# Reordering the operand sums and halves of a seven-product matmul layer, moving some to GpSimd, and loading its first output weights later

## The chip, the cores and the metric

The kernel runs on one core of a Trainium2 chip. The core has a matrix engine (TensorE, PE in the profile, with its weight loads as PEld), three engines for elementwise work (VectorE or DVE, ScalarE or ACT, GpSimd or POOL), and SyncE (SP), whose queue issues the DMAs here. Each engine runs its own instructions in program order and waits on semaphores for the others. The metric is the time of one execution in microseconds (us), the median of several.

## The reference

Three stages follow one another: decayed linear attention, then two feed-forward layers over all 3072 tokens. Everything is float32.

```python
def _attn_ref(q, k, v):                    # 4 x 8 heads x 768 x 64
    for t in range(S):
        state = gamma * state + k[:, :, t] (x) v[:, :, t]
        y[:, :, t] = scale * q[:, :, t] @ state

def _moe_ref(x, w_in, w_out):              # 512 -> 2048 -> 512
    h = x @ w_in
    return (h * np.cos(h)) @ w_out

def _moe2_ref(x, w_gate, w_val, w_out):    # 512 -> 1536 -> 512
    g = x @ w_gate
    silu = g * (1.0 / (1.0 + np.exp(-g)))
    return (silu * (x @ w_val)) @ w_out
```

## The kernel before

Attention and the first feed-forward layer are interleaved and take the first 615 us; the change does not touch them. The tokens are cut into six blocks of 512. Float32 matmuls are done in three passes: each operand is split into a rounded high half (written by ScalarE) and the low half that is left (written by VectorE as a subtraction), and high x high, low x high and high x low are added up in PSUM.

The second layer, from line 680 on, works on pairs of token blocks, three pairs in all, and uses a scheme of seven products in place of eight for a product of 2x2 blocks. The operands of the seven products P1 to P7 are the blocks B11, B21 and B22 themselves and four combinations T1 to T4. The combinations are made in place, one from the other, by subtractions (`g_sum`, line 718): T1 replaces B11's place (slot 0), T2 replaces T1's, T3 goes to slot 1, T4 to slot 2 and needs T2. So the sums have an order, and a place may only be overwritten once its earlier content was split. `g_split` writes the high halves on ScalarE (line 725) and the low halves on VectorE (line 727); with the default `qs` both do it for two chunks, so one call is two instructions on each engine.

The work of a pair runs over 12 *halves* t (36 over all pairs). A half is seven input products of six matmuls each, in the order P1, P2, P4 of the half before, P5, P6, P3, P7 (line 680, `product`). Its results are read out of PSUM: P1 and P5 are copied by ScalarE (857, 874), P6 too (884), and VectorE adds P2, P3 and P7 to these copies (862, 888, 899). Line 899 reads the bank X after P7. P4 of the same half, which runs as the third product of the next half, adds to that bank and so has to wait for line 899. Then ScalarE's sigmoid and VectorE's multiplication (700, 701, 703) form the gated activation in a `raw` tile.

Four halves make a *group* (nine groups, numbered c = 0 to 8, three to a pair; `last` is 8). While the input products of group c run, the output products of group c - 1 (`out_event`, line 766, 14 of six matmuls each, two for each of seven operands) are put between them: `queue` hands one out after P4, P6 and P3, and after P7 in the second and fourth half. Their results are added up by ScalarE or VectorE (775, 777). After the last half the output products of group 8 follow one another without input products between them: the *tail*.

What the change moves is the hand-written placing of `g_sum` and `g_split` in this interleaving: `at(t, name)` is called after the product `name` of half t, h is the half's number in its group, and g = c - 1 is the group whose operands are being made. `one` and `two` name the first and the second of a group's two chunks. Operand work of the token side (`x_sum`, `x_hi`, `x_lo`, lines 631 to 641) is placed by `x_plan`, and falls mainly around the start of each pair, groups 3 and 6.

The weights of the input products come half by half by DMA (`fetch_half`, line 658) in two parts of 1024 and 768 KB: part 0 may be loaded early, part 1 waits for P4 of the half two before. The weights of the output products come in pieces of 512 KB (`fetch_wo`, line 669) into three buffers. All DMAs are issued by SP in program order; the order of these calls in the loop is the order of its queue. The last output products of the first layer, two units, run between the products of the first half (`outs`).

Of the kernel before, what the change touches and what calls it, by code (L numbers as in the profile page):

```python
# [16 lines left out]
ALU = mybir.AluOpType  # L17
# [20 lines left out]
GQ = 2  # L38
# [54 lines left out]
def fused(ctx: ExitStack, tc: tile.TileContext, qkv, w1, w2, consts, out):  # L93
    nc = tc.nc
# [555 lines left out]
    def fetch_half(t, part):  # L650
        if t < len(halves):
            p, q, half = halves[t]
            if part:
                place = Place(w2pool[0], f"b{t % 2}")
                wh[t, part] = place, place.tile([P, 3, 2, 256], "wh")
            else:
                wh[t, part] = want([P, 4, 2, 256], "wh")
            nc.sync.dma_start(out=wh[t, part][1].bitcast(F32), in_=w2d[3 * q + half][part])
# [5 lines left out]
    def fetch_wo():  # L664
        g, n = divmod(next_wo[0], len(ORDER))
        if g < len(groups2):
            next_wo[0] += 1
            wo[g, n] = gpool.tile([P, GQ, 2, 256], F32R, tag="g", name="wo")
            nc.sync.dma_start(
                out=wo[g, n].bitcast(F32).rearrange("p q a c -> p q (a c)"),  # L670
                in_=wod[groups2[g][1]][ORDER.index(order_of(g)[n])],
            )
# [38 lines left out]
    def raw_of(g, qi, slot):  # L711
        p, r = groups2[g]
        return raw[p, GQ * r + qi][1].bitcast(F32)[:, slot]

    def g_sum(g, name, qs=range(GQ)):
        dst, x, y = {"T1": (0, 1, 0), "T2": (0, 3, 0), "T3": (1, 3, 1), "T4": (2, 2, 0)}[name]
        for i in qs:
            nc.vector.tensor_tensor(out=raw_of(g, i, dst), in0=raw_of(g, i, x), in1=raw_of(g, i, y), op=ALU.subtract)  # L718

    def g_split(g, name, qs=range(GQ)):  # L720
        if (g, name) not in opnd:
            opnd[g, name] = want([P, GQ, 2, T], "go")
        t, slot = opnd[g, name][1], SLOT[name]
        for i in qs:
            nc.scalar.activation(out=t[:, i, 0], in_=raw_of(g, i, slot), func=AF.Copy)  # L725
        for i in qs:
            nc.vector.tensor_tensor(  # L727
                out=t[:, i, 1], in0=raw_of(g, i, slot), in1=t[:, i, 0].bitcast(F32), op=ALU.subtract
            )
        if name == "T4":  # L730
            p, r = groups2[g]
            for i in qs:
                raw[p, GQ * r + i][0].give()
# [53 lines left out]
    def second_layer():  # L787
        def flush(n=0):
            for f in later[:len(later) - n]:
                f()  # L790
            del later[:len(later) - n]

        def last_of(t, name):
            p, q, half = halves[t]
            if (q, half) == (M2 // 2 - 1, 1):
                xo[p, PIECES[name][2]][0].give()

        def p4(t):
            x = pst.pop(("X", t))
            n = len(later)  # L800
            product(t, "P4", x, False)
            last_of(t, "P4")
            take_c(t, 1, 0, x)
            flush(len(later) - n)

        queue = []
        both, one, two = range(GQ), range(1), range(1, GQ)
        last = len(groups2) - 1

        def at(t, name):  # L810
            c, h = divmod(t, 2 * GQ)
            g = c - 1
            if name == "P4" and h == 0 and g >= 0:
                queue.extend((g, k) for k in range(14))
                g_split(g, "B21")
            if g >= 0:
                for step, *args in {
                    (0, "P3"): [(g_sum, g, "T1"), (g_split, g, "T1")],
                    (1, "P6"): [(g_sum, g, "T2"), (g_split, g, "T2")],
                    (2, "P2"): [(g_split, g, "B22")],  # L820
                    (2, "P7"): [(g_sum, g, "T3"), (g_split, g, "T3")],
                    (3, "P6"): [(g_sum, g, "T4"), (g_split, g, "T4")],
                }.get((h, name), []):
                    step(*args)
            if c < last:
                if (h, name) == (3, "P7"):
                    g_split(c, "B11")
            else:
                for step, *args in {
                    (2, "P7"): [(g_split, c, "B11", one), (g_sum, c, "T1", one)],  # L830
                    (3, "P2"): [(g_split, c, "T1", one)],
                    (3, "P4"): [(g_split, c, "B21", one), (g_sum, c, "T2", one)],
                    (3, "P5"): [(g_split, c, "T2", one), (g_sum, c, "T3", one)],
                    (3, "P6"): [(g_split, c, "B22", one), (g_sum, c, "T4", one)],
                    (3, "P3"): [(g_split, c, "B11", two), (g_split, c, "T3", one)],
                    (3, "P7"): [(g_sum, c, "T1", two), (g_split, c, "T1", two), (g_split, c, "T4", one)],
                }.get((h, name), []):
                    step(*args)
            if queue and name in ("P4", "P6", "P3") + (("P7",) if h % 2 else ()):
                out_event(*queue.pop(0))  # L840

        for t, (p, q, half) in enumerate(halves):
            x_steps = x_plan.get(t, [])

            def prepare(n):
                for _ in range(n):
                    for step, *args in x_steps.pop(0) if x_steps else []:
                        step(*args)

            def event(name, ps, start):  # L850
                product(t, name, ps, start)
                last_of(t, name)

            X = pst["X", t] = ps_h.tile([P, T], F32, tag="h", name="X")
            event("P1", X, True)
            p1 = tile_t("p1")
            nc.scalar.activation(out=p1, in_=X, func=AF.Copy)
            flush()
            prepare(1)
            Y = ps_a.tile([P, T], F32, tag="a", name="Y")  # L860
            event("P2", Y, True)
            nc.vector.tensor_tensor(out=p1, in0=Y, in1=p1, op=ALU.add)
            take_c(t, 0, 0, p1)
            fetch_half(t + 1, 0)
            prepare(1)
            at(t, "P2")
            if t:
                p4(t - 1)
            fetch_half(t + 1, 1)
            at(t, "P4")  # L870
            Z = ps_a.tile([P, T], F32, tag="a", name="Z")
            event("P5", Z, True)
            p5 = tile_t("p5")
            nc.scalar.activation(out=p5, in_=Z, func=AF.Copy)
            flush()
            prepare(1)
            if outs:
                outs.pop(0)()
            prepare(1)
            at(t, "P5")  # L880
            event("P6", X, False)
            wh[t, 0][0].give()
            u2 = tile_t("u2")
            nc.scalar.activation(out=u2, in_=X, func=AF.Copy)
            prepare(1)
            at(t, "P6")
            event("P3", Z, False)
            nc.vector.tensor_tensor(out=u2, in0=Z, in1=u2, op=ALU.add)
            take_c(t, 0, 1, u2)
            prepare(1)  # L890
            if outs:
                outs.pop(0)()
                for _ in range(3):
                    fetch_wo()
            flush()
            prepare(1)
            at(t, "P3")
            event("P7", X, False)
            nc.vector.tensor_tensor(out=p5, in0=X, in1=p5, op=ALU.add)  # L899
            take_c(t, 1, 1, p5)  # L900
            while x_steps:
                prepare(1)
            at(t, "P7")
        p4(len(halves) - 1)
        flush()
        assert not queue
        for k in range(14):
            out_event(last, k)
            for step, *args in {
                0: [(g_split, last, "B21", two)],  # L910
                1: [(g_sum, last, "T2", two), (g_split, last, "T2", two)],
                3: [(g_sum, last, "T3", two), (g_split, last, "B22", two)],
                5: [(g_split, last, "T3", two), (g_sum, last, "T4", two)],
                7: [(g_split, last, "T4", two)],
            }.get(k, []):
                step(*args)

# [7 lines left out]
    o2, o3, two = (ps_o, "o2"), (ps_o, "o3"), [(ps_a, "a")] * 2  # L925
# [11 lines left out]
    for i in range(CPB):  # L937
        attn_at[21 + 2 * i], attn_at[22 + 2 * i] = scores_of(8 + i), [(attn_both, 8 + i)]
        for j in range(3, NB):
            n, c = 2 * M1 + (j - 3) * M1 + 4 * i, j * CPB + i  # L940
# [20 lines left out]
    for p in range(1, NB // 2):  # L961
        t = p * M2 - 1
# [15 lines left out]
    with tc.manual_schedule():  # L978
# [73 lines left out]
        for a in (  # L1052
# [3 lines left out]
            name, c = a.rstrip("0123456789"), int(a.lstrip("abcdefghijklmnopqrstuvwxyzUy"))  # L1056
# [117 lines left out]
```

## Time and profile before

| | |
|---|---|
| median of 3 runs | 1165.63 us (1165.4 to 1167.32) |
| the profiled execution's own time | 1165.12 us |
| its span in the profile | 1163.3 us |
| PE busy | 1134.7 us (98%) |
| DVE busy | 797.9 us (69%) |
| ACT busy | 629.2 us (54%) |
| POOL busy | 107.5 us (9%), none of it after 600 us |

The time is that of one execution; the span is what lies between the first and the last instruction in its profile. Busy time is the time in which an engine had an instruction running. A timeline row gives the start, the length, the engine, the line, what was written from what, and how many instructions were merged into the row; in brackets is how long the engine sat idle before it and what ended that. Starts of TensorE's rows are the surer measure, since matmuls overlap and their ends are modelled.

### The profile page before, as it was taken

How to read it: one execution, taken by the hardware profiler on the slowest of the kernel's cores; microseconds unless marked ns; L12 is line 12 of the kernel's file. 1: busy time of each engine (PE TensorE's matmuls, PEld its weight loads, DVE VectorE, ACT ScalarE, POOL GpSimd, SP SyncE). 2: the span in 40 equal slices, each digit the busy share in tenths (PEclk: the TensorE clock that was granted, in tenths of full speed). 3: DMA queues.
4: the chain of work that ended last, by engine and by line, in shares of the span. 5: the costliest groups of instructions: out<-in, count | busy, mean ns of one | idle time of the engine just before them, and what ended most of it. 6: DMA issues, size and time to landing. Idle time of an engine off the chain costs nothing.

```text
span 1163.3 us, 16548 instructions
## 1 busy us (share of the span) xinstructions
PE 1134.7 (98%) x6424; PEld 922.3 (79%) x6424; DVE 797.9 (69%) x1334; ACT 629.2 (54%) x954; POOL 107.5 (9%) x98
## 2 busy tenths in 40 slices
PE   8899999999999999999999999999999999999998
PEld 5688878888888888878887788787878787878776
DVE  6866765367676677776756457787756887666677
ACT  5858974457676767668754344333344343344341
POOL 3611221012111211100000000000000000000000
PEclk9999999999999999999999999999999999999999
DMA  9517833245897698598694546675566675664534
GB/s 357 214 37 267 329 145 110 73 143 200 328 352 262 246 365 321 195 368 328 224 346 159 212 179 236 217 289 196 204 231 221 231 275 185 219 220 171 207 108 163
DMA packets 62814, 265.59 MB, mean 228 GB/s; under 512 B 6288, under 2 KB 6544, under 8 KB 47120
## 3 DMA queue, kind: packets, MB, share of 16 engines
q1 hardware_dynamic: 62736, 264.53, 62.0%
q8 instruction: 51, 0.84, 0.3%
q14 instruction: 27, 0.22, 0.1%
HBM read 208.41 MB, written 56.10 MB: 227 GB/s over the span
## 4 chain that ended last, share of the span: by engine, by line
PE 81%; DVE 8%; ACT 6%; DMA 3%; issue 2%; POOL 1%; SPq 0%; DVEq 0%; ACTq 0%; POOLq 0%
PE h L455 20%; PE o L541 20%; PE X L680 14%; PE Z L680 7%; PE oX L766 7%; PE oZ L766 5%; PE Y L680 3%; DVE go L727 2%; PE y L377 2%; ACT rw L166 2%; PE sc L336 1%; DVE acc L777 1%; DMA cst<-in_consts_dram 1%; PE y L369 1%; DMA qkv<-in_qkv_dram 1%
## 5 line engine op out<-in xcount | busy, mean ns | idle before, releaser
L455 PE MATMUL h<-x,w 128*128 128x512 f32 x780 | 191.4, 394 | 1.8 <-ACT w L133 0.8
L541 PE MATMUL o<-g,w 128*128 128x512 f32 x780 | 187.7, 389 | 1.0 <-DVE x L136 1.0
L541 PEld LDWEIGHTS o<-g,w 128*128 128x128 f32 x780 | 146.2, 188 | 31.8 <-issue 1.4
L455 PEld LDWEIGHTS h<-x,w 128*128 128x128 f32 x780 | 144.2, 188 | 34.1 <-ACT w L133 1.2
L680 PE MATMUL X<-xo,wh 128*128 128x512 f32 x576 | 145.7, 390 | 1.3 <-DVE p L899 1.3
L680 PEld LDWEIGHTS X<-xo,wh 128*128 128x128 f32 x576 | 108.0, 188 | 24.9 <-DVE p L899 2.1
L766 PE MATMUL oX<-go,wo 128*128 128x512 f32 x432 | 110.8, 393 | 1.3 <-ACT go L725 1.2
L727 DVE TENSOR_TENSOR go<-raw,go 128x512 fp32r<-128x512 f32 x126 | 81.6, 688 | 29.2 <-ACT go L725 27.8
L766 PEld LDWEIGHTS oX<-go,wo 128*128 128x128 f32 x432 | 81.9, 190 | 19.9 <-ACT go L725 2.1
L498 ACT ACTIVATE n<-h 128x512 int32<-128x512 f32 x96 | 56.9, 592 | 72.3 <-PE h L455 71.5
L725 ACT ACTIVATE go<-raw 128x512 fp32r<-128x512 f32 x126 | 73.9, 625 | 34.8 <-DVE raw L718 31.2
L455 PE MATMUL h<-x,back 128*128 128x512 f32 x372 | 91.0, 393 | 0.0
L541 PE MATMUL o<-g,back 128*128 128x512 f32 x372 | 89.4, 389 | 0.0
L166 ACT ACTIVATE rw<-rw,above 128x1024 uint16<-128x1024 uint32 x34 | 89.3, 2626 | 0.0
L680 PE MATMUL X<-x,wh 128*128 128x512 f32 x288 | 76.4, 402 | 12.3 <-DVE p L899 9.6
L541 PEld LDWEIGHTS o<-g,back 128*128 128x128 f32 x372 | 69.8, 188 | 14.5
L455 PEld LDWEIGHTS h<-x,back 128*128 128x128 f32 x372 | 68.9, 188 | 15.2 <-issue 0.3
L766 PE MATMUL oZ<-go,wo 128*128 128x512 f32 x312 | 79.1, 390 | 0.0
L680 PEld LDWEIGHTS X<-x,wh 128*128 128x128 f32 x288 | 54.6, 192 | 26.7 <-issue 9.2
L680 PE MATMUL Z<-xo,wh 128*128 128x512 f32 x288 | 73.1, 389 | 0.0
L766 PEld LDWEIGHTS oZ<-go,wo 128*128 128x128 f32 x312 | 58.9, 189 | 12.5
L680 PEld LDWEIGHTS Z<-xo,wh 128*128 128x128 f32 x288 | 54.1, 188 | 11.3
(675 smaller groups left out, 1646.6 us busy)
## 6 DMA issues: line engine op xcount, KB each, us to landing
wh<-w2d SPq DMA_DIRECT2D x36, 1024.0 KB, 5.9
rw<-in_w_dram SPq DMA_DIRECT2D x34, 1024.0 KB, 7.2
wo<-wod SPq DMA_DIRECT2D x63, 512.0 KB, 3.7
back<-w1d SPq DMA_DIRECT2D x31, 1024.0 KB, 7.2
wh<-w2d SPq DMA_DIRECT2D x36, 768.0 KB, 4.7
w2d<-parts SPq DMA_DIRECT2D x12, 1024.0 KB, 5.5
xo<-x2d SPq DMA_DIRECT2D x19, 512.0 KB, 6.7
w1d<-w SPq DMA_DIRECT2D x9, 1024.0 KB, 4.8
```

The costliest lines, as they stand in the source:

```text
L166: nc.scalar.activation(out=self.raw.bitcast(U16)[:, :, 2], in_=self.raw[:, :, 0].bitcast(U32), func=AF.Identity, scale=2.0**-29, bias=above,)
L336: nc.tensor.matmul(out=ps_t[c, half][c0:c0 + HALF, i, k0:], lhsT=qk[r0:r0 + D, 1, p0 + k0:p0 + k0 + HALF], rhs=qk[r0:r0 + D, 0, p0 + k0:p0 ...
L369: nc.tensor.matmul(out=y[bank][D * half:D * half + D, slot, :], lhsT=states[c % B][r, h // 2, :], rhs=qk[r, 0, (h // 2) * C:(h // 2 + 1) * C],
L377: nc.tensor.matmul(out=y[bank][D * half:D * half + D, slot, :], lhsT=kv[:, 1, h * D:(h + 1) * D], rhs=s_t[c][:, h % 2, h // 2, :], start=f ...
L455: nc.tensor.matmul(out=ps, lhsT=w[:, a, k * P:(k + 1) * P], rhs=x[:, b, k, :], start=n == 0, stop=n == len(order) - 1,)
L498: nc.scalar.activation(out=n, in_=h, func=AF.Identity, scale=TURN)
L541: nc.tensor.matmul(out=o_t[0][i], lhsT=w[:, a, i * P:(i + 1) * P], rhs=g[:, b, :], start=first and n == 0, stop=last and n == 2,)
L680: nc.tensor.matmul(out=ps, lhsT=w[:, a, k * P:(k + 1) * P], rhs=x[:, b, k, :], start=start and n == 0, stop=n == len(order) - 1, skip_grou ...
L725: nc.scalar.activation(out=t[:, i, 0], in_=raw_of(g, i, slot), func=AF.Copy)
L727: nc.vector.tensor_tensor(out=t[:, i, 1], in0=raw_of(g, i, slot), in1=t[:, i, 0].bitcast(F32), op=ALU.subtract)
L766: nc.tensor.matmul(out=ps, lhsT=w[:, i, a, d * P:(d + 1) * P], rhs=x[:, i, b, :], start=start and m == 0, stop=m == len(order) - 1, skip_g ...
L777: nc.vector.tensor_tensor(out=e[:, c], in0=ps[:, c], in1=e[:, c], op=ALU.add)
```

## The change

Three things are changed in the second layer, and nothing in what is computed.

- In every group the sums and splits of the operands are called at other places of the interleaving. T1's sums go from after P3 to after P5 of the first half and its split from there to after P7, behind line 899. T2's sums go one product forward; B22's split goes from the third half into the second, behind its line 899. T4's sums go from the fourth half to the third, T3's sums and split go from behind the third half's line 899 to ahead of it, and T4's split goes two products forward.
- In the last group, whose own operands are made during its last half and in the tail, seven of the eight single sums are issued to GpSimd in place of VectorE (all but T1's of the second chunk), and the splits of B22, T3 and T4 of the first chunk go into the tail.
- The first three pieces of output weights are loaded in the third half (t = 2) behind both parts of the fourth half's weights, instead of in the first half.

```diff
-    def g_sum(g, name, qs=range(GQ)):
+    def g_sum(g, name, qs=range(GQ), engine=nc.vector):
...
-            nc.vector.tensor_tensor(out=raw_of(g, i, dst), in0=raw_of(g, i, x), in1=raw_of(g, i, y), op=ALU.subtract)
+            engine.tensor_tensor(out=raw_of(g, i, dst), in0=raw_of(g, i, x), in1=raw_of(g, i, y), op=ALU.subtract)
...
                 queue.extend((g, k) for k in range(14))
-                g_split(g, "B21")
             if g >= 0:
                 for step, *args in {
-                    (0, "P3"): [(g_sum, g, "T1"), (g_split, g, "T1")],
-                    (1, "P6"): [(g_sum, g, "T2"), (g_split, g, "T2")],
-                    (2, "P2"): [(g_split, g, "B22")],
-                    (2, "P7"): [(g_sum, g, "T3"), (g_split, g, "T3")],
-                    (3, "P6"): [(g_sum, g, "T4"), (g_split, g, "T4")],
+                    (0, "P4"): [(g_split, g, "B21")],
+                    (0, "P5"): [(g_sum, g, "T1")],
+                    (0, "P7"): [(g_split, g, "T1")],
+                    (1, "P5"): [(g_sum, g, "T2")],
+                    (1, "P6"): [(g_split, g, "T2")],
+                    (1, "P7"): [(g_split, g, "B22")],
+                    (2, "P4"): [(g_sum, g, "T4")],
+                    (2, "P5"): [(g_sum, g, "T3")],
+                    (2, "P6"): [(g_split, g, "T3")],
+                    (3, "P4"): [(g_split, g, "T4")],
...
-                    (2, "P7"): [(g_split, c, "B11", one), (g_sum, c, "T1", one)],
-                    (3, "P2"): [(g_split, c, "T1", one)],
-                    (3, "P4"): [(g_split, c, "B21", one), (g_sum, c, "T2", one)],
-                    (3, "P5"): [(g_split, c, "T2", one), (g_sum, c, "T3", one)],
-                    (3, "P6"): [(g_split, c, "B22", one), (g_sum, c, "T4", one)],
-                    (3, "P3"): [(g_split, c, "B11", two), (g_split, c, "T3", one)],
-                    (3, "P7"): [(g_sum, c, "T1", two), (g_split, c, "T1", two), (g_split, c, "T4", one)],
+                    (2, "P7"): [(g_split, c, "B11", one), (g_sum, c, "T1", one, nc.gpsimd)],
+                    (3, "P2"): [(g_split, c, "T1", one), (g_sum, c, "T2", one, nc.gpsimd)],
+                    (3, "P5"): [(g_split, c, "B21", one), (g_sum, c, "T3", one, nc.gpsimd)],
+                    (3, "P6"): [(g_split, c, "T2", one), (g_sum, c, "T4", one, nc.gpsimd)],
+                    (3, "P3"): [(g_split, c, "B11", two)],
+                    (3, "P7"): [(g_sum, c, "T1", two), (g_split, c, "T1", two)],
...
             fetch_half(t + 1, 1)
+            if t == GQ:
+                for _ in range(3):
+                    fetch_wo()
             at(t, "P4")
...
                 outs.pop(0)()
-                for _ in range(3):
-                    fetch_wo()
...
                 0: [(g_split, last, "B21", two)],
-                1: [(g_sum, last, "T2", two), (g_split, last, "T2", two)],
-                3: [(g_sum, last, "T3", two), (g_split, last, "B22", two)],
-                5: [(g_split, last, "T3", two), (g_sum, last, "T4", two)],
-                7: [(g_split, last, "T4", two)],
+                1: [(g_sum, last, "T2", two, nc.gpsimd)],
+                2: [(g_split, last, "T2", two)],
+                3: [(g_sum, last, "T3", two, nc.gpsimd), (g_split, last, "B22", one)],
+                4: [(g_split, last, "B22", two)],
+                5: [(g_sum, last, "T4", two, nc.gpsimd), (g_split, last, "T3", one)],
+                6: [(g_split, last, "T3", two)],
+                7: [(g_split, last, "T4", one)],
+                8: [(g_split, last, "T4", two)],
```

## Rows read from the trace of the kernel before

**Rows 1.** The page, busy time of each engine (us, share, instructions).

```profile
PE 1134.7 (98%) x6424; PEld 922.3 (79%) x6424; DVE 797.9 (69%) x1334; ACT 629.2 (54%) x954; POOL 107.5 (9%) x98
```

**Rows 2.** TensorE's waits from 600 us on: total, times, longest us.

```profile
PE X L680 <- DVE p L899: 10.9, 9, 2.7
PE X L680 <- DMA wh<-w2d: 2.7, 1, 2.7
```

**Rows 3.** Timeline around the first half of group 1.

```profile
676.50 1.52 PE L680 MATMUL X<-x,wh 128*128 128x512 f32 x6
...
677.43 1.30 DVE L727 TENSOR_TENSOR go<-raw,go 128x512 fp32r<-128x512 f32 x2
677.86 1.52 PE L680 MATMUL Y<-x,wh 128*128 128x512 f32 x6
...
679.25 0.68 DVE L899 TENSOR_TENSOR p<-X,p 128x512 f32<-128x512 f32 x1
...
679.99 1.66 PE L680 MATMUL X<-xo,wh 128*128 128x512 f32 x6 [0.60 <-DVE p L899]
...
681.48 1.52 PE L766 MATMUL oZ<-go,wo 128*128 128x512 f32 x6
```

**Rows 4.** Timeline around the first half of group 3.

```profile
793.97 1.52 PE L680 MATMUL Y<-x,wh 128*128 128x512 f32 x6
...
795.54 1.29 DVE L727 TENSOR_TENSOR go<-raw,go 128x512 fp32r<-128x512 f32 x2 [0.15 <-ACT go L725]
...
797.35 0.68 DVE L899 TENSOR_TENSOR p<-X,p 128x512 f32<-128x512 f32 x1
...
801.02 1.52 PE L680 MATMUL Z<-xo,wh 128*128 128x512 f32 x6
```

**Rows 5.** Timeline of TensorE around the first half of group 6.

```profile
970.17 1.52 PE L680 MATMUL Y<-xo,wh 128*128 128x512 f32 x6
...
978.65 1.54 PE L680 MATMUL Z<-xo,wh 128*128 128x512 f32 x6
```

**Rows 6.** Stretches after two waits: busy by engine, PEclk, DMA share, GB/s.

```profile
798.10:801.00 2.90, 2.82 (x12) 2.36 (x13) 1.98 (x3) 1.68 (x3) 0.00 (x0) 1.00 0.85 294
974.30:978.70 4.40, 4.32 (x13) 3.46 (x14) 1.98 (x3) 1.68 (x3) 0.00 (x0) 0.64 0.92 307
```

**Rows 7.** TensorE's timeline, 636 to 650; line 669 from 632 to 634.

```profile
637.91 1.52 PE L680 MATMUL X<-xo,wh 128*128 128x512 f32 x6
...
647.93 1.53 PE L680 MATMUL Z<-xo,wh 128*128 128x512 f32 x6
...
L669 SPq DMA_DIRECT2D wo<-wod x3: 449/509/600, 632.3 to 633.6; - x3
...
DMA to landing us min/median/max: 4.7/5.3/5.9
```

**Rows 8.** Timeline of TensorE around the end of the last half.

```profile
1127.35 1.52 PE L680 MATMUL Z<-x,wh 128*128 128x512 f32 x6
...
1142.79 1.53 PE L766 MATMUL oZ<-go,wo 128*128 128x512 f32 x6
```

**Rows 9.** Third halves: a stretch (group 2), VectorE and TensorE timeline (group 1).

```profile
751.00:764.70 13.70, 13.70 (x62) 11.36 (x61) 8.25 (x14) 4.10 (x7) 0.00 (x0) 1.00 0.49 174
...
706.16 0.69 DVE L899 TENSOR_TENSOR p<-X,p 128x512 f32<-128x512 f32 x1
...
708.68 1.52 PE L680 MATMUL X<-xo,wh 128*128 128x512 f32 x6
```

**Rows 10.** First layer: timeline from 41 us; lines 174, 304: ns min/median/max, starts.

```profile
41.04 1.73 DVE L174 SCALAR_TENSOR_TENSOR f<-rw,f 128x1024 int32<-128x1024 int32 x1
...
41.65 2.02 POOL L304 TENSOR_TENSOR qkv<-qkv,cst 128x512 f32<-128x512 f32 x1
...
L174 DVE SCALAR_TENSOR_TENSOR f<-rw,f x34: 1217/1220/1726, 17.2 to 569.3; 128x1024 int32<-128x1024 int32 x34
...
L304 POOL TENSOR_TENSOR kv<-kv,cst x12: 1036/1042/2031, 164.6 to 413.0; 128x512 f32<-128x512 f32 x12
```

## Prediction

> **What bounds the kernel now.** I read the page first: TensorE is busy 1134.7 of 1163.3 us [rows 1], so only its pauses can be won back, and a change that moves additions between VectorE and GpSimd is worth just what it takes from those pauses. Next came the list of waits, cut to the second layer, from 600 us on. The reader should see two names there: TensorE waits for line 899 nine times, 10.9 us together, and once for a DMA, 2.7 us [rows 2]. Last I took the timeline around each wait, to see what line 899 stood behind and how late the matmuls after the wait began.
>
> A product is six matmuls, and products start 1.36 us apart when nothing stops them (676.50 to 677.86) [rows 3]. That pitch turns each wait into a whole loss, the slow matmuls behind it included. In the ordinary case the second product after the one at 677.86 should start 2.72 us later, at 680.58; the row says 681.48, a loss of 0.90 us [rows 3]. The product between them is P4 of the half before, which may not write its bank until line 899 has read it. Line 899 starts at 679.25, although its product P7 is followed by the next half's first from 676.50 on, since VectorE takes T1's two sums (line 718) and, from 677.43, their two low halves (line 727) first.
>
> Of the nine waits one belongs to the first half of each group 1 to 8 and one to the end. Groups 3 and 6 start a new pair of token blocks and do that pair's operand work as well. There three pitches became 7.05 us (793.97 to 801.02) [rows 4] and 8.48 us (970.17 to 978.65) [rows 5], against 4.08: losses of 2.97 and 4.40. The two waits were equally long; the difference is the clock, granted 1.00 after the one and 0.64 after the other [rows 6]. The six ordinary groups lose 6 x 0.90 = 5.40. Around the DMA wait five products took 10.02 us (637.91 to 647.93) [rows 7]: 10.02 - 4 x 1.36 = 4.58 over four pitches. At the end of the last half seven pitches took 15.44 us (1127.35 to 1142.79) [rows 8], against 9.52: 5.92 lost. Together 5.40 + 7.37 + 4.58 + 5.92 = 23.27 us, the most that the change can win.
>
> **First part: sums and halves reordered.** In the first half of a group the low halves of T1 go behind line 899 and T1's sums go ahead of P6. In an ordinary group that takes four VectorE instructions out of the way. They start 0.6 us apart (795.54 to 797.35 holds two low halves and one eviction) [rows 4], so line 899 comes up to 2.4 us earlier and is held only by P7. P4 began 0.74 us after line 899 started (679.25 to 679.99) [rows 3]; with 899 at about 676.8, P4 could start at 677.5, and its turn is 679.22. All 5.40 us go.
>
> In groups 3 and 6 the queue is full of the pair's work, and the sums, moved forward, still stand between P5 and line 899: one of the pair's low halves stands ahead of them and waits for ScalarE, so they can't fill that gap. Only the low halves leave, with their idle time: 2 x 0.6 + 0.15 = 1.35 us. Line 899 then starts at 797.35 - 1.35 = 796.00, P4 0.74 later at 796.74, and its turn is 793.97 + 1.36 = 795.33: 1.4 remain, with 0.15 for the slow restart (0.90 lost, 0.77 waited in the ordinary case) some 1.55. The gain is 2.97 - 1.55 = 1.42, and 4.40 - 1.55 = 2.85 if the clock stays up. Bounds: no wait left (7.37), or 1.43 more lost each where the clock falls (4.40 - 2.97).
>
> What is late next: T1's low halves are not wanted before P5's output product in the second half, five products on. T2's split stays and its sums come sooner. B22's split moves ahead of the next half's first evacuation on ScalarE, whose reader is several products off. I cost these at nothing; were that cover gone, each microsecond would cost one. The third half gets more in front of its line 899: sums of T4 and T3 and the low halves of T3, six instructions, 3.6 us, while B22's two leave it. In the second group VectorE was busy there 8.25 of 13.70 us, which leaves 5.4 idle, and in the first, line 899 at 706.16 stands 2.5 us ahead of the P4 at 708.68, 1.8 more than the 0.74 it wants [rows 9]. I cost it at nothing; bounds 0 and 2.
>
> **Second part: output weights later.** The three loads of 512 KB are issued from 632.3 to 633.6, ahead of the next half's 1024 KB of weights in SP's queue, and land 4.7 to 5.9 us after issue [rows 7]. Without them that megabyte takes the place of the first two, the second of which, issued at 632.9, lands 5.3 later, at about 638.2. TensorE wants it at 637.91 + 1.36 = 639.27: 1.1 us to spare. I take all 4.58; the bounds are 0 and 4.58. The loads go behind both parts of the fourth half's weights in SP's queue, hence past four more issues and the wait for the P4 whose turn is 639.27 + 2 x 1.36 = 641.99. Their first reader is the first output product, fifteen products or 20 us after that P4, and the fifth half's weights, issued behind them, have twelve, 16 us. So this costs nothing; were it not hidden, one wait of 2.7 [rows 2].
>
> **Third part: the last group on GpSimd.** In and just before the last half VectorE loses four sums, three low halves (of B22, T3 and T4) go into the output tail, and T4's sums of the group before go to the third half. These are what line 899 stood behind. GpSimd does nothing else in this layer. A sum of 128x512 is not in its rows, but a product of that size took 1.04 to 2.03 us [rows 10]; with three instructions at 0.6 the chain from one operand's low half through sum and high half to the next one's needs some 4 us at most, and each operand is given three products or more, 4.1. In the tail each split is issued four products, 5.4 us, ahead of its use. So the 5.92 us go, except for what the two engines cost each other. A two-input VectorE instruction took 1.73 us instead of 1.22 beside a GpSimd product that took 2.02 [rows 10]. Two such delays of 0.5 in front of the last line 899, which has 0.6 to spare (P7 ends one pitch before P4's turn, 1.36 - 0.74), make 0.4; the second tail product, whose bank is evicted behind T1's last sum and split, may cost as much again: I take 0.8, an estimate. Bounds: 0, and four sums at 0.5 with 1.4 of slow clock, 3.4.
>
> The Trainium skill, "SBUF — State Buffer", section "Who interferes with whom", speaks against this part: a VectorE instruction with both inputs in SBUF and a GpSimd instruction that reads SBUF lock each other out, and the later one waits for the whole of the first. By that rule each of four sums could hold VectorE up for its whole length, and the end would gain some 2 us instead of 5.1, which makes about 1149.4 (an estimate). The rows agree that both engines are slowed, VectorE by 0.5 and not by a whole GpSimd instruction.
>
> **The sum.** 5.40 + 1.42 + 2.85 + 4.58 + (5.92 - 0.8) = 19.37 us. The profiled execution took 1165.12 us, its span 1163.3 and 1.8 around it; 1165.12 - 19.4 = 1145.7. It lay 0.5 below the median of 1165.63, so I forecast 1146.2.
>
> **Rivals.**
> - No wait remains: the pair's work runs earlier as well, and GpSimd disturbs nothing. 1165.6 - 23.3 = 1142.4. For it: each half before has less VectorE work. Against: the full queue above.
> - GpSimd and VectorE hinder each other, or the clock falls after the waits left in groups 3 and 6: up to 2.6 us (3.4 - 0.8) and 2.9 us (2 x 1.43) more, about 1149 for one of them. For it: the slowed pair [rows 10], and 0.64 after one wait and 1.00 after its twin [rows 6].
> - The weights are late anyway, since the first layer's last stores stand ahead of them in either order: 4.6 less, 1150.8. The margin of 1.1 speaks against it.
> - Slower: the six instructions in front of the third half's line 899 make it late. It decides from 1.8 us of delay on; at the price of the wait in group 3 (2.97) in eight groups, 23.8 is lost against 19.4 won: 1170. The idle 5.4 us speak against it.
> - The order makes no difference, because line 899 was held by something that the trace puts down wrongly: little would come but the weights' and the end's gain, 4.6 + 5.1: 1156. That the low halves fill VectorE up to one eviction before line 899 [rows 3, 4] speaks against it.
>
> **How the numbers follow.** Forecast 0.58 (its own range 1144.5 to 1148), no wait 0.10, hindrance or clock 0.20, late weights 0.06, no effect of the order 0.02, slower 0.04. From 1142.8 to 1150.5 leaves out most of the last three and half of the no-wait case, under 2 in 10. A measurement here tells about 0.2%, 2.3 us, from no change: faster 0.95, same 0.02, slower 0.03 (the slower case need not reach that bound in all eight groups).
>
> **What would show it.** Right: in the list of waits line 899 has two or three entries, of 1.5 us or less, at the first halves of groups 3 and 6 and perhaps at the very end; the DMA wait is gone; GpSimd has 7 instructions of line 718; products in the ordinary groups keep their 1.36 us throughout. Wrong: a wait of P4 in a third half, waits for line 725 or 727 by output products, a new DMA wait within 25 us of the layer's start, line 727 well over 0.69 us in the last half, or a granted clock of 0.6 to 0.7 after the waits that are left.

## The result, and the profile after

The changed kernel takes 1146.62 us (median of four runs, 1145.68 to 1148.29), the kernel before 1166.11 beside it: a ratio of 0.9833, 95% interval 0.9816 to 0.9850. The forecast was 1146.2. A second set of runs on another chip gave 1146.88 and 0.9827 [0.9813, 0.9842]. The profiled execution took 1146.71 us with a span of 1144.7, 18.6 less than before. The second layer alone became 19.6 us shorter: its first product starts at 616.91 (before 615.92), so 547.4 us before and 527.8 after lie behind that start; the first layer, which is not changed, was 1.0 longer in this execution.

The page, busy time of each engine, to set against [rows 1]:

```profile
PE 1127.8 (99%) x6424; PEld 920.6 (80%) x6424; DVE 797.1 (70%) x1327; ACT 626.7 (55%) x954; POOL 117.6 (10%) x105
```

VectorE has seven instructions less and GpSimd seven more, yet VectorE is busy only 0.8 us less, where seven sums of 0.68 would be 4.8. Most of that gap, 2.4 us, is found in the last half, below. TensorE's waits from 600 us on, to set against [rows 2]:

```profile
PE X L680 <- DVE p L903: 2.8, 3, 1.0
PE oX L766 <- DVE acc L777: 0.3, 1, 0.3
```

Line 899 is now line 903 (898 to 905 in the kernels of the experiments). Its nine waits have become three, two of 1.03 and one of 0.72, and the wait for a DMA is gone. The list before had one entry more than [rows 2] show, the wait of an output product near the end for the split of T4 (line 725), which the forecast counted in the loss of the end:

```profile
PE oX L766 <- ACT go L725: 1.2, 1, 1.2
```

It is gone as well, and one short wait of an output product for line 777 is new.

The timeline around the first half of group 1, against [rows 3]:

```profile
666.01 1.28 DVE L718 TENSOR_TENSOR raw<-raw 128x512 f32<-128x512 f32 x2
...
673.12 0.69 DVE L903 TENSOR_TENSOR p<-X,p 128x512 f32<-128x512 f32 x1
...
674.28 1.52 PE L680 MATMUL Y<-x,wh 128*128 128x512 f32 x6
...
675.03 1.29 DVE L727 TENSOR_TENSOR go<-raw,go 128x512 fp32r<-128x512 f32 x2 [1.22 <-ACT go L725]
...
675.64 1.52 PE L680 MATMUL X<-xo,wh 128*128 128x512 f32 x6
```

T1's sums now start 7 us ahead of line 903, and its low halves (line 727) stand behind it. That line starts at 673.12, and P4 comes exactly two pitches after the product at 672.92 and one after the product at 674.28, at 675.64: nothing is lost. The other five ordinary groups look the same, and the list of waits holds none of them.

The timeline around the first half of group 3, against [rows 4]:

```profile
784.35 1.23 DVE L641 TENSOR_TENSOR xo<-xs,xo 128x1024 fp32r<-128x1024 f32 x1 [1.13 <-ACT xo L637]
785.50 1.29 DVE L718 TENSOR_TENSOR raw<-raw 128x512 f32<-128x512 f32 x2
...
788.51 1.52 PE L680 MATMUL Y<-x,wh 128*128 128x512 f32 x6
...
790.24 0.68 DVE L903 TENSOR_TENSOR p<-X,p 128x512 f32<-128x512 f32 x1
...
791.06 1.63 PE L680 MATMUL X<-x,wh 128*128 128x512 f32 x6 [1.03 <-DVE p L903]
...
793.90 1.52 PE L680 MATMUL Z<-xo,wh 128*128 128x512 f32 x6
```

Three pitches took 793.90 - 788.51 = 5.39 us, against 4.08: 1.31 lost, where 2.97 were lost before and 1.55 were forecast. Line 903 follows an unbroken queue, and the queue starts late: VectorE stands idle 1.13 us for a high half of the pair (line 637), with T1's two sums behind the waiting instruction. Group 6 waits as long, and its clock did not fall this time. The stretches after the waits in groups 3 and 6, with the granted clock ahead of the last two numbers, against [rows 6]:

```profile
790.90:794.00 3.10, 2.94 (x13) 2.46 (x14) 1.88 (x5) 2.65 (x5) 0.00 (x0) 1.00 0.89 291
963.50:966.60 3.10, 2.87 (x13) 2.39 (x14) 1.88 (x4) 2.64 (x5) 0.00 (x0) 1.00 0.91 277
```

The weights, against [rows 7]: the load that took the place of the first output weights, its landing, and then the timeline of the products that want it and of SP's queue.

```profile
L658 SPq DMA_DIRECT2D wh<-w2d x1: 547/547/547, 633.3 to 633.3; - x1
...
DMA to landing us min/median/max: 5.7/5.7/5.7
```

```profile
638.92 1.52 PE L680 MATMUL X<-xo,wh 128*128 128x512 f32 x6
640.28 1.52 PE L680 MATMUL X<-x,wh 128*128 128x512 f32 x6
...
644.92 1.59 SPq L669 DMA_DIRECT2D wo<-wod  x3
```

The load is issued at 633.3, has landed at 639.0, and its product starts in its turn at 640.28, 1.3 us later. The output weights go at 644.92, and nobody waits for them.

The end of the last half, against [rows 8], with GpSimd's sums and VectorE's low halves from 1110 on one by one:

```profile
1107.35 0.68 DVE L865 TENSOR_TENSOR p<-Y,p 128x512 f32<-128x512 f32 x1
1108.07 1.07 DVE L703 TENSOR_TENSOR raw<-p,raw 128x512 f32<-128x512 f32 x1
...
1106.97 1.62 POOL L718 TENSOR_TENSOR raw<-raw 128x512 f32<-128x512 f32 x1 [541.17 <-DVE go L727]
...
1110.05 1.29 POOL L718 TENSOR_TENSOR raw<-raw 128x512 f32<-128x512 f32 x1 [1.47 <-DVE go L727]
...
1110.29 1.61 DVE L727 TENSOR_TENSOR go<-raw,go 128x512 fp32r<-128x512 f32 x1 [0.31 <-ACT go L725]
...
1111.31 1.73 POOL L718 TENSOR_TENSOR raw<-raw 128x512 f32<-128x512 f32 x1
...
1111.82 1.77 DVE L727 TENSOR_TENSOR go<-raw,go 128x512 fp32r<-128x512 f32 x1
...
1117.53 1.52 PE L766 MATMUL oX<-go,wo 128*128 128x512 f32 x6
...
1119.04 0.68 DVE L903 TENSOR_TENSOR p<-X,p 128x512 f32<-128x512 f32 x1
...
1119.77 1.67 PE L680 MATMUL X<-x,wh 128*128 128x512 f32 x6 [0.72 <-DVE p L903]
...
1123.10 1.66 PE L766 MATMUL oX<-go,wo 128*128 128x512 f32 x6 [0.27 <-DVE acc L777]
1124.59 2.88 PE L766 MATMUL oZ<-go,wo 128*128 128x512 f32 x12
```

From 1117.53 to 1124.59 four pitches took 7.06 us, against 5.44: 1.62 lost, where 5.92 were lost and 0.8 forecast. The two low halves beside GpSimd's two sums take 3.30 us, from 1110.29 to 1113.59; without a sum beside them such a pair takes 1.30 [rows 3]. Lines 727 and 718 over the layer, min/median/max in ns:

```profile
L718 POOL TENSOR_TENSOR raw<-raw x7: 1285/1302/1732, 1107.0 to 1125.8; 128x512 f32<-128x512 f32 x7
...
L727 DVE TENSOR_TENSOR go<-raw,go x126: 676/685/1772, 660.9 to 1134.9; 128x512 fp32r<-128x512 f32 x126
```

### The profile page after: what moved, and what is told of

Its sections match the earlier page's. It is cut to its first block, busy times and chain, and to the rows that moved or that the text cites. A ratio compares the mean times of both kernels' runs of the same rounds, so it can differ in the third digit from the quotient of the medians.

```text
span 1144.7 us, 16528 instructions
## 1 busy us (share of the span) xinstructions
PE 1127.8 (99%) x6424; PEld 920.6 (80%) x6424; DVE 797.1 (70%) x1327; ACT 626.7 (55%) x954; POOL 117.6 (10%) x105
## 4 chain that ended last, share of the span: by engine, by line
PE 86%; DVE 5%; ACT 5%; DMA 2%; issue 1%; POOL 0%; SPq 0%; DVEq 0%; POOLq 0%
PE h L455 21%; PE o L541 20%; PE X L680 15%; PE Z L680 8%; PE oX L766 7%; PE oZ L766 6%; PE Y L680 4%; PE y L377 2%; ACT rw L166 2%; DMA rw<-in_w_dram 2%; PE sc L336 1%; PE y L369 1%; DVE go L727 1%; DVE acc L777 1%; ACT w L133 1%
## 5 line engine op out<-in xcount | busy, mean ns | idle before, releaser
L727 DVE TENSOR_TENSOR go<-raw,go 128x512 fp32r<-128x512 f32 x126 | 84.6, 709 | 35.0 <-ACT go L725 34.6
L680 PE MATMUL X<-x,wh 128*128 128x512 f32 x288 | 73.4, 390 | 2.8 <-DVE p L903 2.8
L718 POOL TENSOR_TENSOR raw<-raw 128x512 f32<-128x512 f32 x7 | 10.1, 1449 | 551.2 <-DVE go L727 551.2
```

The source lines that it names most:

```text
L680: nc.tensor.matmul(out=ps, lhsT=w[:, a, k * P:(k + 1) * P], rhs=x[:, b, k, :], start=start and n == 0, stop=n == len(order) - 1, skip_grou ...
L727: nc.vector.tensor_tensor(out=t[:, i, 1], in0=raw_of(g, i, slot), in1=t[:, i, 0].bitcast(F32), op=ALU.subtract)
```

## The experiments

Two measures stand in the table: the median with its ratio to the kernel before on the same chip (1166.07 to 1166.88 there), and the loss in the second layer of the profiled execution. The loss is the sum, over all pauses and slow stretches, of the time from one matmul's start to the next less the ordinary 1.36/6 us. The kernel before loses 23.48 by it (23.27 by the prediction's rows), the changed one 4.28. A repetition of the changed kernel that shared its chip with some of the experiments:

> The changed kernel once more, beside the next kernels on the same chip: 1146.6, with waits of 1.0 us at the first halves of groups 3 and 6 and 0.7 and 0.3 at the end.

| kernel | median us | ratio [95%] | loss, us |
|---|---|---|---|
| changed, again | 1146.88 | 0.9827 [0.9813, 0.9842] | 4.29 |
| T1's move alone | 1155.47 | 0.9904 [0.9890, 0.9918] | 13.76 |
| first part alone | 1153.70 | 0.9894 [0.9879, 0.9909] | 10.72 |
| second part alone | 1162.58 | 0.9966 [0.9952, 0.9980] | 20.34 |
| third part alone | 1165.26 | 0.9994 [0.9982, 1.0007] | 23.26 |
| first and second, no third | 1147.42 | 0.9838 [0.9824, 0.9851] | 5.58 |
| changed, sums back on VectorE | 1145.91 | 0.9827 [0.9812, 0.9843] | 4.09 |
| changed, pair's low halves later | 1144.46 | 0.9807 [0.9794, 0.9821] | 1.77 |
| that, on VectorE, T4 in the tail, eviction first | 1144.42 | 0.9806 [0.9791, 0.9820] | 1.83 |
| the last but T4 back in the half | 1144.28 | 0.9811 [0.9798, 0.9825] | 1.56 |
| the last but one with the tail's sums on GpSimd | 1143.05 | 0.9798 [0.9785, 0.9812] | 0.21 |

**T1's move alone.** The kernel before with one entry of the table changed:

```diff
-                    (0, "P3"): [(g_sum, g, "T1"), (g_split, g, "T1")],
+                    (0, "P5"): [(g_sum, g, "T1")],
+                    (0, "P7"): [(g_split, g, "T1")],
```

> The kernel before with T1's move alone (its sums behind P5, its split behind P7 of the first half); everything else as before. Theory: this move alone takes away all that the first part won in the groups, 10.2 us, 1156; the DMA wait and the end's loss stay, and no new wait comes in the second halves. Rival: the other moves are needed as well, because T1's split now stands in the second half, where T2's sums and split already are: waits for line 899 appear at the second halves and 2 to 5 us of the gain are lost, 1158 to 1161.

The loss falls by 9.72 us, the median by 10.7. TensorE's waits from 600 us on:

```profile
PE X L680 <- DVE p L900: 4.3, 3, 1.8
...
PE oX L766 <- ACT go L725: 1.2, 1, 1.2
```

The nine waits are three, as in the changed kernel, but the one at the end is 1.8 long: groups 1 to 8 are settled by this entry alone, up to 0.2 us in each of groups 3 and 6 (1.47 are lost there, 1.27 by the same measure in the changed kernel), and the end is not. T1's sums and its split were not moved apart from each other.

**First part alone.** The kernel before with the whole table of the groups from the change.

> The kernel before with the first part alone (the table for groups 0 to 7); the last group's own table and the tail are unchanged and all sums are on VectorE. Theory: the waits of the ordinary first halves go, those of groups 3 and 6 shrink to 1.0 us each as in the changed kernel (10.2 us), and the last half loses the sums and split of T4 of group 7 in front of its output product and of line 899 as well, so most of the end's 5.9 us goes without GpSimd: about 15 less, 1151. Rival: the end needs the third part; only the wait for T4's split goes there, 12.4 less, 1153.8. Second rival: line 899 was not held by T1's sums and halves: 1160 or more.

```profile
PE X L680 <- DVE p L903: 3.5, 3, 1.4
...
PE oX L766 <- DVE acc L777: 0.9, 1, 0.9
```

Compared with T1's move alone the loss falls by 3.04 more. 2.99 of that lies at the end, where 2.87 are lost (1.71 and 1.16) in place of 5.86 (2.14 and 3.72); groups 3 and 6 lose 0.40 less together, the DMA wait 0.35 more (5.10, 4.75). So half of the end's loss goes without the third part, not most of it, and the time is that of the first rival. The last half no longer has T4's sums and split of group 7 in it, and the wait for line 725 is gone; but the entries for T2, T3 and B22 are in this kernel as well, and T4's was not tried by itself.

**Second part alone.** The kernel before with the three calls of fetch_wo moved as in the change.

> The kernel before with the second part alone (the first output weights loaded in the third half). Theory: the DMA wait and the slow clock behind it go and nothing else moves; 4.58 us less, about 1161.5, all nine waits for line 899 stay. Rival: the weights of the third half are late anyway because the stores of the first layer stand ahead of them; the wait stays and the time is 1166.

```profile
PE X L680 <- DVE p L900: 10.9, 9, 2.7
PE oX L766 <- ACT go L725: 1.2, 1, 1.2
```

The DMA wait is gone, and with it 4.53 us, but the loss falls by only 3.14 in this profile. The missing part is in group 3: after a wait of 2.68 us, as long as before, the granted clock fell there, which it had not in [rows 6]. The same columns:

```profile
793.70:797.00 3.30, 3.25 (x8) 2.61 (x9) 1.99 (x3) 1.40 (x3) 0.00 (x0) 0.51 0.90 305
```

0.51 is close to the level of 1.2 GHz where 1.00 is 2.4; group 3 lost 4.52 here instead of 2.93. On top of the first part, where no such long wait is left beside it, the move is worth its whole price (next but one).

**Third part alone.** The kernel before with the engine argument of g_sum, the last group's table and the tail from the change.

> The kernel before with the third part alone (sums of the last group on GpSimd, three splits into the tail). Theory: T4's sums and split of group 7 still stand in the last half, so the wait of an output product for line 725 stays in part and the wait for the last line 899 shrinks: 2 to 4 us less, about 1163. Rival: the third part is what removes the end's loss: 5 us less, 1161.

```profile
PE oX L766 <- ACT go L725: 1.7, 2, 1.2
```

No difference that can be measured. In the profile the wait for the last line 898 is gone, the output products still wait for T4's split, and the end loses 4.25 us (3.98 and 0.27) in place of 5.84; but the DMA wait cost 5.99 in that execution in place of 4.53, and its ten runs spread from 1161.96 to 1168.02. The forecast of 5.12 us for this part does not hold for it alone in any case.

**First and second part without the third.** Both edits above together.

> The kernel before with the first and second part and without the third (last group's table and tail as before, all sums on VectorE). Theory: waits of 1.4 and 0.9 at the end as in e2_order against 0.7 and 0.3 with the third part, so the third part is worth 1.1 to 1.5: 1148. Rival: the third part, forecast to win 5.1, is worth that much: 1151 to 1152.

The list of waits is that of the first part alone without the DMA wait. The loss falls from 10.72 to 5.58, so the weights are worth 5.14 us here, the whole DMA wait. The end loses 2.85, as in the first part alone (2.87). What the third part adds in the changed kernel is 5.58 - 4.28 = 1.30 us by the loss, and 0.5 to 0.8 by the medians, where the intervals of the ratios overlap.

**The sums back on VectorE.** The changed kernel, in seven places:

```diff
-"T1", one, nc.gpsimd)
+"T1", one, nc.vector)
```

> The changed kernel with the seven sums of the last group on VectorE, at the same places. Theory: GpSimd gains nothing, since a VectorE instruction with two SBUF inputs waits out the GpSimd sum beside it (line 727 took 1.6 to 1.8 us there and not 0.69, some 2.4 us in all, as much as the four sums of 0.6 that it took away): the same as the changed kernel within 1 us, 1146. Rival: GpSimd is what frees VectorE ahead of the last line 899; with 2.4 us back in the queue the last wait grows from 0.7 to 3 us with a slow clock behind it: 1149 to 1151.

1145.91 against 1146.88 on another chip, with the same ratio of 0.9827: the engine makes no difference that can be measured. The end loses 1.19 us here and 1.53 by the same measure with GpSimd. Line 727 over the layer, and the timeline of the pair of low halves that took 3.30 us and of the last P4:

```profile
L727 DVE TENSOR_TENSOR go<-raw,go x126: 681/685/696, 660.3 to 1134.4; 128x512 fp32r<-128x512 f32 x126
```

```profile
1110.18 1.28 DVE L727 TENSOR_TENSOR go<-raw,go 128x512 fp32r<-128x512 f32 x2
...
1118.85 1.66 PE L680 MATMUL X<-x,wh 128*128 128x512 f32 x6 [0.35 <-DVE p L903]
```

No low half is slow any more, and P4 waits 0.35 us where it waited 0.72. VectorE does four sums more ahead of that line 903, 4 x 0.6 = 2.4 us, and still reaches it sooner.

**The wait in groups 3 and 6.** The changed kernel with the pair's low halves of T3 one product later:

```diff
-            [(x_lo, p, "B22")], [], [(x_sum, p, "T3"), (x_hi, p, "T3")], [(x_lo, p, "T3")],
-            [(x_hi, p, "T4")], [(x_lo, p, "T4")],
+            [(x_lo, p, "B22")], [], [(x_sum, p, "T3"), (x_hi, p, "T3")], [],
+            [(x_lo, p, "T3"), (x_hi, p, "T4")], [(x_lo, p, "T4")],
```

> The changed kernel, with the pair's low half of T3 taken behind the group's sums of T1 and not ahead of them, in groups 3 and 6. Theory: VectorE stood idle 1.1 us in front of that low half, waiting for ScalarE; with the sums in the gap line 903 comes 1.1 us sooner, both waits of 1.0 go, 2 x 1.3 = 2.6 less: 1144.0. Rival: these waits come from the amount of VectorE work in the half and not from its order; the time stays at 1146.6.

VectorE's timeline in group 3, and the wait list:

```profile
783.86 1.28 DVE L718 TENSOR_TENSOR raw<-raw 128x512 f32<-128x512 f32 x2
785.07 1.23 DVE L641 TENSOR_TENSOR xo<-xs,xo 128x1024 fp32r<-128x1024 f32 x1
...
789.75 0.68 DVE L903 TENSOR_TENSOR p<-X,p 128x512 f32<-128x512 f32 x1
```

```profile
PE X L680 <- DVE p L903: 0.7, 1, 0.7
...
```

T1's sums now run while ScalarE makes the high half, the idle 1.13 us is gone, and so are both waits: the loss falls by 2.5 us and the median by 2.4. It was not the amount of work ahead of line 903, but an instruction that waited at the head of VectorE's queue.

**Toward the best version.** Three kernels put the findings together. The first has that edit, all sums on VectorE, and on top of these T4's first sum in the tail and one eviction of output ahead of the last group's steps:

```diff
+                if (h, name) == (3, "P7"):
+                    out_event(*queue.pop(0))
...
-                    (3, "P6"): [(g_split, c, "T2", one), (g_sum, c, "T4", one, nc.vector)],
+                    (3, "P6"): [(g_split, c, "T2", one)],
...
-                4: [(g_split, last, "B22", two)],
+                4: [(g_sum, last, "T4", one), (g_split, last, "B22", two)],
```

> The changed kernel with the reorder of the run before, all sums on VectorE, the last output product of group 7 evicted ahead of T1's last sum and split, and T4's sum of the first chunk moved into the tail. Theory: the four waits that are left (1.0, 1.0, 0.4, 0.3) are all order on VectorE's queue and go, with their slow restarts some 3.6 us less than the changed kernel on VectorE (1145.9): 1142.4, what is left once all waits of the layer are gone. Rival: the tail's VectorE work has no room for more, and a wait of an output product for line 727 takes their place: 1144 or more.

Both waits at the end are gone, and a new one took their place. TensorE's timeline and SP's queue:

```profile
1126.99 2.14 SPq L780 DMA_DIRECT2D out_dram<-acc  x2
1129.22 0.88 SPq L669 DMA_DIRECT2D wo<-wod  x2
...
1133.11 3.21 PE L766 MATMUL oX<-go,wo 128*128 128x512 f32 x13 [1.13 <-DVE acc L777]
```

The trace names line 777, but the output weights were issued at 1129.22, behind two stores that wait for VectorE's evictions, and landed 3.75 us later, at 1132.97: the wait is for them, and 1144.42 us is no gain on the 1144.46 of the reorder alone. The line 777 that ended last there is not what the product reads: in the third kernel below the same product starts at 1131.52, before that line 777 does at 1131.72. The second kernel takes T4's sum back into the half:

> The run e7_best with T4's sum of the first chunk back in the last half. Theory: e7_best lost its last microsecond in the tail, where each sum that is added makes VectorE's evictions later; with one sum less there the wait of 1.1 in the tail goes, the last line 903 waits 0.4 again as in the changed kernel on VectorE, and the second tail product does not: 1143.7, some 0.7 less than e7_best. Rival: the wait in the tail is one for a DMA that the order of evictions has moved, and stays: 1144.4 or more.

It waits 0.35 us for the last line 903 (905 there) and 0.48 for the same weights, and gains nothing that can be measured: the rival holds. The third is the first with the four sums of the tail on GpSimd, behind the last line 903:

> The run e7_best with the tail's four sums on GpSimd and those of the last half on VectorE. Theory: GpSimd costs VectorE in lock-outs about what it takes over, as in the last half, so the tail's wait of 1.1 stays or moves: 1144.4 within 1. Rival: in the tail many VectorE instructions read PSUM and are not held up, GpSimd's sums are free there and the wait goes: 1143.3.

```profile
L718 POOL TENSOR_TENSOR raw<-raw x4: 1297/1747/1844, 1119.8 to 1124.6; 128x512 f32<-128x512 f32 x4
```

TensorE's list of waits in the second layer is empty: the load goes out at 1127.96, lands at 1131.37 and is wanted at 1131.52. So the rival holds. 1143.05 us is the fastest of all the kernels, 3.6 to 3.8 below the changed one, although the ratios of these last three can't be told apart by their intervals.

## Why the prediction was right, and where its terms were off

**Ordinary groups**, 5.40 forecast: all six lost 0.87 to 0.93 by their matmul starts before and nothing after. T1's move alone shows that its reorder does it.

**Groups 3 and 6**, 1.42 + 2.85 forecast: 1.31 are left in each where 1.55 were expected, so 1.66 and 3.09 came (the matmul starts give 1.27 left in either group). P4 started 1.19 us behind its turn in group 3 in place of 1.4, because line 903 came 0.3 us sooner than in the sum. T1's move alone won 9.72 us by loss, against 9.67 forecast for these two points together. The reason given, that the sums can't fill the idle time because a low half waits ahead of them, is shown by the experiment that moves that low half. The clock, which could have taken the gain of group 6 back, stayed at 1.00.

**Output weights**, 4.58 forecast: the DMA wait's whole price came, 4.53 alone (where the fallen clock in group 3 took 1.59 of it back) and 5.14 on top of the first part. The margin was 1.3 us, 1.1 forecast. The loads' own reader waited for nothing.

**The end**, 5.92 - 0.8 = 5.12 forecast: 5.92 - 1.62 = 4.30 came. The mis-sized term is the price of two engines beside each other, sized at two delays of 0.5 us for VectorE in front of the last line 903. There were three, 2.4 us together: two low halves were 0.9 and 1.1 late (1.61 and 1.77 in place of 0.69), line 703 by 0.4. Line 727 well over 0.69 us in the last half was one of the prediction's own signs of being wrong, and for this term it was right. The bound that was given, 3.4, was not reached. Not all of the 1.62 is this price: the second tail product, on which the sum had put half of its 0.8, waits as long with every sum on VectorE (0.30) as with GpSimd (0.27).

The 0.5 was misread from [rows 10]. They show the GpSimd product that started after line 174's slow instruction; the one that ran before it was left out:

```profile
39.94 1.75 POOL L312 TENSOR_TENSOR qkv<-qkv,cst 128x512 f32<-128x512 f32 x1
```

It ended at 41.69. Line 174's instruction started at 41.04 and ended at 42.77, 1.08 after that, where it takes 1.22 alone; the GpSimd product from 41.65 on ended 0.90 after line 174's, at 43.67, where one takes 1.04 alone. So each ended nearly its whole usual length after the other engine's earlier instruction, and the 0.5 was only what had been left of that one. The rows from 1110.05 on show the same: the first low half ends 0.55 us after the first sum, the second sum 1.14 after that, the second low half 0.55 after the second sum. The four take 3.54 together, against 2 x 1.30 + 2 x 0.69 = 3.98 end to end. So these instructions ran in turns, and hardly side by side.

The Trainium skill, "SBUF — State Buffer", section "Who interferes with whom", has a VectorE instruction with two SBUF inputs and a GpSimd instruction that reads SBUF exclude each other, the later one waiting for the whole of the first. The trace agrees, with the ends 0.55 and 1.14 us apart, and the prediction's sentence against it, "by 0.5 and not by a whole GpSimd instruction", was wrong. The section has an instruction with one SBUF input go free; line 865, which reads PSUM and SBUF, took its usual 0.68 beside a sum at 1107.35.

**Which part won the end.** The prediction booked all 5.12 on the third part. That step fails, although the same paragraph names T4's sums of the group before, which are in the first part's table: the order of the groups before wins 3.0 of it (first part alone against T1's move alone), the third part 1.3 on top, and moving sums to GpSimd none of that, since they can go back to VectorE at no cost. What is left of the third part is its order, low halves into the tail: with all sums on VectorE the last group's new places take the loss from 5.58 to 4.09. Of the two that offset each other, GpSimd's help and hindrance, neither was measured by itself.

**What did not come.** The six instructions in the third half did no harm: in group 1 line 903 started 2.4 us ahead of P4, the margin of 2.5 before [rows 9] almost unchanged. VectorE's timeline and TensorE's there:

```profile
701.79 0.68 DVE L903 TENSOR_TENSOR p<-X,p 128x512 f32<-128x512 f32 x1
...
704.20 1.52 PE L680 MATMUL X<-xo,wh 128*128 128x512 f32 x6
```

The sum: 2 x 1.31 + 1.62 = 4.24 of 23.27 are left, so 19.0 were won against 19.4 forecast. The errors of 0.24 twice and of 0.82 point in opposite directions, and the forecast of 1146.2 came within 0.5 us in part for that reason.

## What to carry to other kernels

Turn each wait into a whole loss, from the pitch of the product starts around it, and then read what the late instruction stood behind on its own engine: an instruction that waits at the head of an in-order queue costs more than several that run. An operation is moved for its deadline, not for its engine; sending sums to GpSimd took 2.4 us off VectorE and cost it as much, and emptied the list of waits only where nothing urgent was left behind it. Where two engines slow each other, look at what the other engine had running before the slow instruction, and not only at what ran beside it. Loads belong in the queue in the order in which they are wanted, and not behind a store that waits for an engine.

## What the runs showed of the hardware that was not expected

- A GpSimd sum and a two-input VectorE addition ran in turns: the addition ended 0.55 us after the sum that had started before it, the sum 1.14 to 1.16 after such an addition (the changed kernel and the fastest one). So 0.69 became 1.61 and 1.77, and 1.30 became 1.62 to 1.84.
- The clock after a wait is not settled by the wait's length. After 2.7 us at the same place of the same order it was granted as 1.00 in one kernel [rows 6] and 0.51 in another (second part alone), and after the changed kernel's waits of 1.03 us it was 1.00. But in the third part alone it fell behind two waits of an output product of 0.53 and 1.18 us, 1.7 us apart:

```profile
1132.70:1136.30 3.60, 3.60 (x10) 2.58 (x9) 3.56 (x7) 0.63 (x2) 0.00 (x0) 0.53 0.00 0
```

- The DMA wait at the start of the second layer cost between 4.53 and 5.99 us in four kernels that issue its loads in the same order.
